# A two-layer MoE chain on one core: a strand's five output products in one go, and the issue order laid out anew

## The chip, the cores and the metric

The kernel runs on one core of a Trainium2 chip. The metric is device time in microseconds (us) for one execution, lower is better. The kernel before has two timed runs with a median of 1358.05 us.

## What is computed

Three stages follow each other. A causal convolution mixes each token with its six predecessors (softmax of seven taps for each of eight heads). Then two feed-forward layers run on 8192 tokens of width 192, with 2048 hidden channels each: `h = x @ w_in`, a function of `h` alone, then `g @ w_out`.

```python
x_unf = x_pad[:, idx, :].reshape(B, S, K, H, group)
out = np.einsum('hk,bskhg->bshg', w, x_unf)       # the convolution
g = h * np.clip(h + 3.0, 0.0, 6.0) / 6.0          # layer 1
P = a[0] + a[1] * h + a[2] * h2 + a[3] * h3       # layer 2
Q = 1.0 + np.abs(b[0]) * np.abs(h) + np.abs(b[1]) * h2
g = P / (Q + 1e-06)
```

## The kernel before

**Tiles and strands.** The tokens are cut into 16 blocks of 512 columns; the last is cut again into two units of 256, so there are 17 units. A unit takes 16 steps (the halves 8), and each step treats 128 hidden channels of a layer: a tile. Every number that enters a product is held as a high part and a low part (`h` and `l` in the tile names), and a product is the sum of three matmuls: high by high, low weight by high, high weight by low. TensorE's 128 rows are used as two halves of 64, called strands: `L` is rows 0 to 63 and `H` rows 64 to 127. Matmuls of the two strands run side by side. TensorE takes all of them from one queue in order, so a matmul that waits holds both strands.

**What happens to a tile.** `product_in` (`mm1` in layer 1, `mm3` in layer 2) makes `h` with nine matmuls of one strand into one of four PSUM banks. ScalarE (ACT), VectorE (DVE) and GpSimd (POOL) work out `g`; `hi1`/`hi2` (lines 953 and 1046, ACT) make its high part `g1h`/`g2h`, and `lo1`/`lo2` (lines 957 and 1052, POOL) its low part `g1l`/`g2l`. `product_out` then adds `g @ w_out` onto two accumulators: `acc..0` for output channels 0 to 127 (A) and `acc..1` for channels 128 to 191 with the low weights (B). For each strand it comes in two pieces: the piece for the high part, which issues A, A, B and needs only the high part, and the piece for the low part, which issues A, B.

**The fences.** Both strands add to the same accumulators, and two row halves must not write a bank at the same time. So where the strand changes on an accumulator, `fence_of` (line 635) puts an empty instruction on SP's queue that waits for the other strand's last matmul, and the first matmul of the new strand waits for that instruction. SP's queue also issues nearly all transfers: weights (`raw`, lines 733 to 737), tokens (`xn`, line 821), copies between partition halves (`X<-X`, `x1_dup` and `x2_dup`, line 894) and results (`out_dram`, lines 1094 and 1099). It is worked off in order too.

**The order.** Nothing of the order is written by hand. `make_plan` enters every operation with an engine, an assumed duration and a due time (`at`; the table `P["OFF"]` shifts it by operation). `Issue.order` plays the operations through a model with queues, rings of buffers and banks, and the instructions are issued by its start times. In that model `CROSS` (375 ns) is the distance that is kept between the strands on an accumulator; a fence takes no time of SP. Some entries on SP stand for several transfers: `load_w` for three (1950 ns), `load_x` for three (2400 ns), and copies and results are entered with 60 ns each. All transfers of an entry are issued at its start, one behind the other. A transfer issued there stands ahead of every fence that is planned later.

**The head.** `warm` runs 29 calls on zeros (5 over all rows, 12 of two matmuls with 512 columns, 12 of two with 192) before the convolution of blocks 0 and 1 (`conv0`, `conv1`), the transposes (`flip0`, `flip1`), and the first layer-1 products.

Of the kernel before, what the change touches and what calls it, by code (L numbers as in the profile page):

```python
# [15 lines left out]
SPAN = 58  # L16
C = 512
# [16 lines left out]
 'WARM': 29,  # L34
 'TH': 0.001,
 'DUP': 2600,
 'WPART': {'c0': 0.0497, 'v0': 0.0414, 'vs': 0.0403, 'h0': 0.2096, 'l0': 1.1533},
 'HEAD': 80.77,
 'TAIL': 205.47,
# [10 lines left out]
 'AHEAD': {'P': 63636833941.194, 'A': 527134343714.242, 'V': 3.0551887163097883e+19, 'G': 0.0, 'S': 999.0},  # L50
 'LOOK': {'P': 108, 'A': 139, 'V': 147, 'G': 63, 'S': 0},
 'BIAS': {'l1': -1.5284, 'dec': -4.5327, 'conv': -5.2656, 'out': -121.8403, 'x2': -83.2364},
 'OFF': {'sq': 2.5051,
         'q1': -34.3348,
         'q2': -49.934,
         'mm3': 1.398,
         'mm1': 2.9299,
         'mm4L': 3.5225,
         'mm4H': 2.7712,
         'tr': 18.9987,  # L60
         'mm2L': 4.3258,
         'mm2H': 5.2665,
         'A': 2.0453,
         't1': 1.7144,
         'u': -19.1188,
         'R': 46.5874,
         'RR': 3.1074,
         'hi2': 4.2135,
         'hi1': -20.696,
         'S': -21.1003,  # L70
         'lo2': 27.916,
         'lo1': -32.6451,
         'q': 7.2528,
         't2': 64.7646,
         't3': -9.1293,
         'w': -9.3652,
         'p2': 2.9972,
         'G': -37.509,
         'g': -9.5099,
         'cv': -34.3227,  # L80
         'x1ah': 45.5678,
         'x1al': -25.3374,
         'x1bh': 11.1259,
         'x1bl': -9.2318,
         'x2ah': -42.7502,
         'x2al': -101.0403,
         'x2mh': -17.8371,
         'x2mc': -53.8528,
         'x2ml': 72.7752,
         'oa': -65.1337,  # L90
         'oc': 11.2138,
         'os': 3.4069,
         'mm2lL': 4.9092,
         'mm2lH': 5.1772,
         'mm4lL': 3.5751,
         'mm4lH': -41.4037,
         '0.mm2L': -41.6908,
         '0.mm2lL': -85.6444,
         '0.mm2H': -21.0061,
         '0.mm2lH': -181.1908,  # L100
         '0.x2mh': -226.4626,
         '0.lo1': -47.901,
         '0.x2ml': 78.7106,
         '0.x2al': -138.5753,
         '0.x2mc': -132.4879,
         '0.mm1': -83.2957,
         '0.hi1': -166.5497,
         '0.g': -29.6109,
         '0.u': -157.145,
         '0.x2ah': -84.5959,  # L110
         'T.sq': -23.8172,
         'T.mm4lL': -110.3747,
         'T.mm4lH': -50.2917,
         'T.x2al': -5.029,
         'T.RR': -35.6781,
         'T.q2': -152.042,
         'T.oa': -153.8478,
         'T.lo2': 97.3004,
         'T.mm3': -180.9259,
         'T.q1': 0.5761,  # L120
         'T.A': -84.0279,
         'T.t3': -194.1138,
         'T.w': -176.0944,
         'T.G': -165.3819,
         'T.x2mh': -25.799,
         'T.x2ml': -100.5773,
         'T.hi2': -113.8752,
         'T.R': -115.1862,
         'T.p2': 21.7375,
         'T.tr': -148.8753,  # L130
         'T.q': -97.9184,
         'T.os': -90.2945,
         'T.mm4L': -58.7026,
         'T.mm4H': -180.8402,
         'T.x2mc': -189.2563,
         'trc': 1.5457,
         'x1d': 26.3031,
         'x2d': -34.7349,
         'x2e': 14.9362,
         '0.x2d': -16.7171,  # L140
         '0.x2e': -175.0551,
         'T.x2d': -72.3839,
         'T.x2e': -115.9305,
         'c.trc': -127.1013,
         'c.cv': 104.2546,
         'c.x1ah': -220.4013,
         'c.x1al': 77.084,
         'c.x1bh': 67.322,
         'c.x1bl': 59.1881,
         'c.x1d': -188.5031},  # L150
 'H1': 2,
 'H2': 3}
# [65 lines left out]

class Issue:
# [3 lines left out]
    CROSS = 375  # L223
# [12 lines left out]
    def lag(self, e, x):  # L236
        if e in "LH" and x in "LH":
            return 0 if e == x else self.CROSS
        p = lambda y: "P" if y in "LH" else y
        return self.DELAY.get(p(e) + p(x), 150)  # L240

    def graph(self):
# [5 lines left out]
        for k, op in enumerate(ops):  # L248
# [10 lines left out]
            assert all(key in written or key[0] == "X" for key in r), op  # L259
            for key in dict.fromkeys((*r, *w)):  # L260
# [19 lines left out]
                if key[0] == "X" and users[key]:  # L280
                    pred.setdefault(users[key][0], False)
# [16 lines left out]
    def order(self):  # L298
# [12 lines left out]
        def from_(k, e):  # L311
            if k in takes:
                return max(ready[k], min(idle[b][e] for b in idle))
            if ops[k][14] and ops[k][14][2]:
                last, x = lock.get(ops[k][14][0], (0.0, e))
                return max(ready[k], last + (self.CROSS if x != e else 0.0))
# [880 lines left out]
```

## Time and profile before

| | us |
|---|---|
| median of 2 runs | 1358.05 |
| lowest and highest | 1355.74, 1360.35 |
| the profiled execution, its own time | 1359.84 |
| its span, first to last instruction | 1358.0 |
| TensorE (PE) busy | 1294.3 |
| DVE, ACT, POOL busy | 1159.9, 1153.6, 1112.2 |

PE counts as busy as soon as one strand is; a matmul's end is modelled, so matmuls that follow each other on one strand overlap in the record. PEld is the loading of weights into the array. PEclk is the share of TensorE's clock that was granted. "SPq L635" as a releaser is a fence.

### The profile page before, as it was taken

To read this page: it belongs to the slowest core of one execution; us is meant where nothing else is said; L and a number is where in the kernel's file an instruction comes from. 1 tells how busy PE (TensorE), PEld (TensorE's weight loads), DVE (VectorE), ACT (ScalarE), POOL (GpSimd) and SP (SyncE) were. 2 spreads that over 40 slices of the span, in tenths; PEclk is the share of its full clock that TensorE was granted. 3 is DMA by queue.
4 is the path that set the end of the run, shared out by engine and by line. 5 is a ranking of instruction groups with operands and counts; after the bars stand their busy time and mean duration, and the time that the engine had idled before them with its cause. 6 is when DMAs were issued, how large, how long until landed. Compare 5 with 4: busy or idle time off the path is not lost.

```text
span 1358.0 us, 31232 instructions
## 1 busy us (share of the span) xinstructions
PE 1294.3 (95%) x11356; PEld 1132.5 (83%) x11356; DVE 1159.9 (85%) x1812; ACT 1153.6 (85%) x2121; POOL 1112.2 (82%) x948
## 2 busy tenths in 40 slices
PE   8888899999999999999999999999998999999998
PEld 6677688888877778888888989788997998999997
DVE  5777798898888979888998989898997998999985
ACT  3566798998888989888998989898997999999974
POOL 2578597898978889788997989898897898998963
PEclk7899999999999999999999999999999999999986
DMA  5443201102020200202012020200202110011010
GB/s 146 123 112 90 68 2 45 21 18 48 1 65 1 50 16 1 64 1 57 10 18 48 9 57 2 57 9 13 54 13 46 19 26 16 14 25 25 5 21 13
DMA packets 74466, 48.58 MB, mean 36 GB/s; under 512 B 43084, under 2 KB 64968, under 8 KB 74312
## 3 DMA queue, kind: packets, MB, share of 16 engines
q1 hardware_dynamic: 74152, 46.42, 14.8%
q8 instruction: 90, 1.47, 0.5%
q14 instruction: 64, 0.52, 0.1%
q10 hardware_dynamic: 160, 0.16, 0.1%
HBM read 20.34 MB, written 6.30 MB: 20 GB/s over the span
## 4 chain that ended last, share of the span: by engine, by line
PE 49%; ACT 21%; DVE 17%; SPq 5%; issue 5%; POOL 2%; DMA 0%; DVEq 0%; ACTq 0%; POOLq 0%
PE acc L628 25%; PE bank L628 23%; DVE T L1005 4%; ACT A L986 3%; ACT T L990 3%; ACT g1h L953 3%; DVE T L1017 2%; DVE S L1032 2%; ACT bank L1027 2%; ACT g2h L1046 2%; ACT A L1022 2%; DVE u L949 2%; DVE bank L1036 2%; ACT S L997 2%; ACT u L945 2%
## 5 line engine op out<-in xcount | busy, mean ns | idle before, releaser
L628 PE MATMUL bank<-X,Ih 64*128 64x512 f32 (+1 forms) x3264 | 926.8, 384 | 10.9 <-DVE T L1017 4.7
L628 PEld LDWEIGHTS bank<-X,Ih 64*128 64x128 f32 x3264 | 551.4, 187 | 67.0 <-DVE T L1017 12.5
L628 PE MATMUL bank<-X,Il 64*128 64x512 f32 (+1 forms) x1632 | 577.6, 379 | 0.0
L628 PE MATMUL acc<-g2h,O 64*128 64x512 f32 (+1 forms) x1728 | 473.0, 387 | 8.8 <-SPq L635 7.6
L628 PE MATMUL acc<-g1h,O 64*128 64x512 f32 (+1 forms) x1536 | 416.3, 381 | 9.7 <-SPq L635 8.9
L957 POOL TENSOR_TENSOR g1l<-u,g1h 128x512 fp32r<-128x512 f32 x240 | 310.8, 1297 | 77.1 <-ACT g1h L953 66.7
L1052 POOL TENSOR_TENSOR g2l<-T,g2h 128x512 fp32r<-128x512 f32 x255 | 330.5, 1298 | 46.4 <-ACT g2h L1046 34.2
L1011 POOL TENSOR_TENSOR S<-A,S 128x512 f32<-128x512 f32 x256 | 331.3, 1298 | 34.4 <-ACT S L997 19.3
L628 PE MATMUL acc<-g2l,O 64*128 64x512 f32 (+1 forms) x1152 | 344.9, 390 | 10.6 <-SPq L635 9.6
L628 PEld LDWEIGHTS acc<-g2h,O 64*128 64x128 f32 x1728 | 310.6, 191 | 27.4 <-SPq L635 9.7
L628 PE MATMUL acc<-g1l,O 64*128 64x512 f32 (+1 forms) x1024 | 303.2, 382 | 4.2 <-SPq L635 4.1
L628 PEld LDWEIGHTS bank<-X,Il 64*128 64x128 f32 x1632 | 293.5, 187 | 13.0
L628 PEld LDWEIGHTS acc<-g1h,O 64*128 64x128 f32 x1536 | 269.9, 186 | 30.7 <-SPq L635 13.3
L1005 DVE SCALAR_TENSOR_TENSOR T<-T,coef,bank 128x512 f32<-128x512 f32 x256 | 190.1, 743 | 47.8 <-ACT A L986 30.5
L628 PEld LDWEIGHTS acc<-g2l,O 64*128 64x128 f32 x1152 | 205.6, 191 | 28.7 <-SPq L635 14.6
L1017 DVE SCALAR_TENSOR_TENSOR T<-T,coef,bank 128x512 f32<-128x512 f32 x256 | 190.4, 745 | 20.5 <-ACT S L997 12.5
L1032 DVE SCALAR_TENSOR_TENSOR S<-S,bank 128x512 f32<-128x512 f32 x256 | 174.5, 683 | 32.3 <-ACT bank L1027 25.9
L990 ACT ACTIVATE T<-bank,coef 128x512 f32<-128x512 f32 x256 | 174.8, 684 | 23.5 <-PE bank L628 21.5
L628 PEld LDWEIGHTS acc<-g1l,O 64*128 64x128 f32 x1024 | 180.2, 185 | 16.9 <-SPq L635 4.5
L1036 DVE SCALAR_TENSOR_TENSOR bank<-T,coef,bank 128x512 f32<-128x512 f32 x256 | 191.7, 749 | 0.2
L949 DVE SCALAR_TENSOR_TENSOR u<-u,bank 128x512 f32<-128x512 f32 x240 | 163.2, 682 | 30.3 <-ACT u L945 26.8
L1041 DVE SCALAR_TENSOR_TENSOR T<-S,bank 128x512 f32<-128x512 f32 x256 | 175.1, 684 | 6.1
(90 smaller groups left out, 1733.7 us busy)
## 6 DMA issues: line engine op xcount, KB each, us to landing
X<-X SPq DMA_DIRECT2D x73, 256.0 KB, 3.3
raw<-in_moe_w_out_dram SPq DMA_DIRECT2D x16, 384.0 KB, 3.2
xn<-in_x_dram SPq DMA_DIRECT2D x28, 192.0 KB, 3.3
out_dram<-ov SPq DMA_DIRECT2D x60, 64.0 KB, 2.0
raw<-in_moe_w_in_dram SPq DMA_DIRECT2D x16, 192.0 KB, 3.6
raw<-in_moe_w_in_dram SPq DMA_DIRECT2D x16, 128.0 KB, 3.2
out_dram<-A SPq DMA_DIRECT2D x15, 128.0 KB, 2.0
raw<-in_moe_w_in_dram SPq DMA_DIRECT2D x16, 64.0 KB, 2.8
```

The source lines that it names most:

```text
L628: return nc.tensor.matmul(out=out, lhsT=lhsT, rhs=rhs, start=start, stop=stop, skip_group_check=True, **k)
L949: stt(out=t, in0=t, scalar=1.0, in1=h1.pop((b, i)), op0=ALU.min, op1=ALU.mult)
L953: act(out=g1[b, i][0], in_=v1[b, i], func=ACTF.Copy)
L957: nc.gpsimd.tensor_tensor(out=g1[b, i][1], in0=v1.pop((b, i)), in1=f32(g1[b, i][0]), op=ALU.subtract)
L990: act(out=tile2(b, i, "T"), in_=h2[b, i], func=ACTF.Copy, scale=coef[:, 3:4])
L1005: stt(out=d["T"], in0=d["T"], scalar=coef[:, 2:3], in1=h2[b, i], op0=ALU.add, op1=ALU.mult)
L1011: (nc.gpsimd if k else nc.vector).tensor_tensor(out=d["S"], in0=d["A"], in1=d["S"], op=ALU.add if k == 1 else ALU.mult)
L1017: stt(out=d["T"], in0=d["T"], scalar=coef[:, 1:2], in1=h2[b, i], op0=ALU.add, op1=ALU.mult)
L1032: stt(out=d["S"], in0=d["S"], scalar=c1, in1=r2[b, i], op0=ALU.add, op1=ALU.mult)
L1036: stt(out=r2[b, i], in0=v2[b, i]["T"], scalar=coef[:, 0:1], in1=r2[b, i], op0=ALU.add, op1=ALU.mult)
L1041: stt(out=d["T"], in0=d["S"], scalar=2.0, in1=r2.pop((b, i)), op0=ALU.subtract, op1=ALU.mult)
L1052: e.tensor_tensor(out=g2[b, i][1], in0=v2.pop((b, i))["T"], in1=f32(g2[b, i][0]), op=ALU.subtract)
```

## The change

`product_out` no longer has a piece for the high and one for the low part. One section issues all five products of a strand for a tile, A, A, A and then B, B, and needs both parts. `CROSS` becomes 212.7 ns, and lags between engines get an extra (`SLACK`: 98.6 ns from PE to another engine, 43.4 ns between others). Each transfer of `load_w` and `load_x` is an operation of its own with 645 ns on SP (weights of `w_out` 420, x with padding 1290), and copies and results are entered with 640, 490 and 430 ns instead of 60. A bank that passes from one engine to another keeps a lag in the model. `WARM` rises from 29 to 44 calls; the 15 more are pairs of 192 columns. The table of due times is new, without the entries that held for the first two and the last unit alone, and so are the rules that say how far an engine may look ahead. The number of products, evictions and vector operations stays as it was.

```diff
- 'WARM': 29,
+ 'WARM': 44,
...
+ 'CROSS': 212.7,
+ 'SLACK': [0, 98.6, 43.4]}
...
+        extra = P["SLACK"][0 if x in "LH" else 1 if e in "LH" else 2] if e != x and e != "S" and x != "S" else 0.0
+        return self.DELAY.get(p(e) + p(x), 150) + extra
...
-        at(t_load, None, "S", 1950, "load_w", *key, r=[("line_d", 0)], w=[("raw", key)], after=3400)
+        for j in range(parts):
+            at(t_load + 0.001 * j, None, "S", 645 if parts == 3 else 420, "load_w", *key, j, r=[("raw", key)] + [("line_d", 0)] * (t_load >= -62),
+               w=[("rl", key, j)], after=3600)
...
-                at(t, pick(z, "mm2" + e), e, o3, "product_out", 0, b, i, y, False, 
-                   d=D, r=[Hi] + [("out" + v, 0, c) for v in "hl" for c in cs], lock=ac, kind="l1")
-                at(t, pick(z, "mm2l" + e), e, o2, "product_out", 0, b, i, y, True, 
-                   d=D, r=[Lo] + [("outh", 0, c) for c in cs], lock=ac, kind="l1")
+                at(t, pick(z, "mm2" + e), e, o5, "product_out", 0, b, i, y,
+                   d=D, r=[Hi, Lo] + [("out" + v, 0, c) for v in "hl" for c in cs], lock=ac, kind="l1")
...
-            at(t, pick(z, ("x2d", "x2d", "x2e")[j]), "S", 60, "x2_dup", b, j, r=need + [X], w=[(f"x2d{j}", b)], after=P["DUP"], kind="x2", d=D)
+            at(t, pick(z, ("x2d", "x2d", "x2e")[j]), "S", 640, "x2_dup", b, j, r=need + [X], w=[(f"x2d{j}", b)], after=P["DUP"], kind="x2", d=D)
...
-        at(-100 + 45 * b if first else t - 8, None, "S", 2400, "load_x", b, r=[("line_d", 0)] if b else [], w=[xk(b)], after=1700)
+        for j in range(3):
+            at((-100 + 45 * b if first else t - 8) + 0.001 * j, None if first else f"ld{j}", "S",
+               645 if j or b * C % 4096 else 1290, "load_x", b, j, r=[xk(b)] + [("line_d", 0)] * (b == 1), w=[("xl", b, j)], after=1700)
...
-        seq = ((0, 0), (1, 128)) if lo else ((0, 0), (0, 256), (1, 128))
...
+        for j, parts in ((0, ((0, 0), (0, 256), (1, 0))), (1, ((0, 128), (1, 128)))):
+            for f, cs in tiles_of(l, u, i):
+                for lo, o in parts:
+                    count[l, u][j] += 1
+                    k = mm(acc[l, u][j], W[l]["O"][row(z), f, o:o + 128], (g1, g2)[l][u, i][lo][row(z), cs],
+                           count[l, u][j] == 1, count[l, u][j] == total[j])
+                    chain(k, fence.pop(j, None))
```

**Where instructions stand.** First PE's queue in the middle of the program, before. `bank` is the bank of a `product_in`; `acc_9011` and `acc_9012` are the A and B accumulators of a unit's layer 2, `acc_9159` and `acc_9160` those of another unit's layer 1; `g1` and `g2` are the layers' values.

```order
L628 MATMUL acc_9011<-g2h,O_129 128x512
L628 MATMUL bank_106<-X,Ih_124 128x512
L628 MATMUL acc_9011<-g2h,O_129 128x512
L628 MATMUL bank_106<-X,Il_125 128x512
L628 MATMUL acc_9012<-g2h,O_129 128x512
L628 MATMUL bank_106<-X,Ih_124 128x512
L628 MATMUL acc_9159<-g1l,O_126 128x512
L628 MATMUL bank_106<-X,Ih_124 128x512
L628 MATMUL acc_9160<-g1l,O_126 128x512
L628 MATMUL bank_106<-X,Il_125 128x512
```

The strand that adds takes the three products of a high part (A, A, B on layer 2) and goes on with the two of a low part of another unit (A, B). Now the same engine, same place, after; here `acc_8927` and `acc_8928` are A and B of layer 2.

```order
L585 MATMUL bank_105<-X,Ih_127 128x512
L585 MATMUL acc_8927<-g2h,O_129 128x512
L585 MATMUL bank_105<-X,Il_128 128x512
L585 MATMUL acc_8927<-g2h,O_129 128x512
L585 MATMUL bank_105<-X,Ih_127 128x512
L585 MATMUL acc_8927<-g2l,O_129 128x512
L585 MATMUL bank_105<-X,Ih_127 128x512
L585 MATMUL acc_8928<-g2h,O_129 128x512
L585 MATMUL bank_105<-X,Il_128 128x512
L585 MATMUL acc_8928<-g2l,O_129 128x512
```

All five products of a tile follow each other on one strand, three on A and then two on B.

Next PE's queue in the head, before: the last of block 2's convolution (`xn,band`) and the first product of layer 1 (`bank_105<-X,Ih_124`); `perm` rows are transposes of block 1.

```order
L874 MATMUL bank_105<-perm,X 128x58
L628 MATMUL bank_107<-xn,band 128x120 x2
L628 MATMUL bank_106<-xn,band 128x96
L628 MATMUL bank_107<-xn,band 128x120
L628 MATMUL bank_106<-xn,band 128x96
L628 MATMUL bank_107<-xn,band 128x120
L628 MATMUL bank_106<-xn,band 128x96 x2
L628 MATMUL bank_107<-xn,band 128x96 x2
L628 MATMUL bank_105<-X,Ih_124 128x512
```

Block 2's convolution stands between block 1's transposes and the first product. After, the same place:

```order
L836 MATMUL bank_105<-perm,X 128x58
L836 MATMUL bank_107<-perm,X 128x58
L836 MATMUL bank_105<-perm,X 128x58 x3
L836 MATMUL bank_107<-perm,X 128x58 x4
L836 MATMUL bank_108<-perm,X 128x58 x9
L585 MATMUL bank_105<-X,Ih_124 128x512
L585 MATMUL bank_105<-X,Il_125 128x512
```

The first product follows the transposes directly, and block 2's convolution has moved behind it.

Last SP's queue in the second half, transfers alone (fences stand between them but are not listed), before:

```order
L894 DMA X<-X 64x2x512 x2
L821 DMA xn<-in_x_dram 64x4x192
L821 DMA xn<-in_x_dram 64x192
L821 DMA xn<-in_x_dram 64x4x192
L894 DMA X<-X 64x2x512 x3
L1094 DMA out_dram<-ov 32x16x32 x4
L1099 DMA out_dram<-A 128x4x64
```

After:

```order
L856 DMA X<-X 64x2x512 x3
L782 DMA xn<-in_x_dram 64x4x192
L782 DMA xn<-in_x_dram 64x192
L782 DMA xn<-in_x_dram 64x4x192
L856 DMA X<-X 64x2x512 x2
L1055 DMA out_dram<-ov 32x16x32 x4
L1060 DMA out_dram<-A 128x4x64
```

The transfers are the same, and no transfer of another kind stands between the three of a block; what can now stand between them are fences.

## Rows read from the trace of the kernel before

**Rows 1.** The page: the span, and the engines' busy time.
```profile
span 1358.0 us, 31232 instructions
...
PE 1294.3 (95%) x11356; PEld 1132.5 (83%) x11356; DVE 1159.9 (85%) x1812; ACT 1153.6 (85%) x2121; POOL 1112.2 (82%) x948
```

**Rows 2.** Windows by stage: us, busy time by engine (instructions), granted clock, DMA share, GB/s.
```profile
680.00:816.00 136.00, 130.80 (x1155) 117.80 (x1153) 119.88 (x181) 121.23 (x224) 115.59 (x98) 0.99 0.16 33
...
1292.00:1358.00 66.00, 60.00 (x508) 56.81 (x508) 44.18 (x67) 37.79 (x69) 35.32 (x31) 0.76 0.06 16
```

**Rows 3.** Everything of line 635, the fences on SP's queue: who waited, us, times.
```profile
L635 SPq EVENT_SEMAPHORE  x1655: 17/17/17, 15.3 to 1353.2; - x184
...
  PEld acc L628: 42.1, 47
  PE acc L628: 30.2, 33
...
  PE bank L628: 4.6, 6
...
  PE bank L1076: 3.0, 2
```

**Rows 4.** Timeline 1031 to 1038 us: start, us, engine, line, tiles, idle before.
```profile
1032.12 1.26 SPq L894 DMA_DIRECT2D X<-X  x2
...
1033.48 2.38 SPq L821 DMA_DIRECT2D xn<-in_x_dram  x3
...
1035.97 0.61 PE L628 MATMUL acc<-g2h,O 64*128 64x512 f32 x1 [3.71 <-SPq L635]
...
1036.38 0.62 PE L628 MATMUL acc<-g2h,O 64*128 64x512 f32 x1
...
1036.81 0.62 PE L628 MATMUL acc<-g2h,O 64*128 64x512 f32 x1
```

**Rows 5.** Timeline 96 to 100 us, the weight loads in front of a fence.
```profile
96.54 0.59 SPq L733 DMA_DIRECT2D raw<-in_moe_w_in_dram  x1
...
97.83 1.34 SPq L735 DMA_DIRECT2D raw<-in_moe_w_in_dram  x1
...
99.29 0.50 PE L628 MATMUL acc<-g2l,O 64*128 64x512 f32 x1 [2.11 <-SPq L635]
```

**Rows 6.** Windows at the lower clock: after a stall, and in the head.
```profile
1036.20:1039.70 3.50, 3.50 (x21) 2.78 (x21) 0.00 (x0) 0.51 (x2) 1.31 (x2) 0.51 0.37 92
...
15.60:39.00 23.40, 20.15 (x134) 18.03 (x133) 13.17 (x29) 9.63 (x20) 5.46 (x7) 0.50 0.55 151
39.00:42.90 3.90, 3.90 (x24) 3.82 (x23) 2.19 (x4) 1.96 (x4) 1.66 (x3) 0.50 0.13 30
```

**Rows 7.** Timeline 700 to 712 us, PE alone: two products of one strand.
```profile
703.74 0.39 PE L628 MATMUL acc<-g2l,O 64*128 64x512 f32 x1
...
703.97 0.39 PE L628 MATMUL acc<-g2h,O 64*128 64x512 f32 x1
```

**Rows 8.** Timeline 0 to 70 us, PE alone: the head.
```profile
1.31 10.83 PE L628 MATMUL warm<-S 128*128 128x512 f32 x58 [1.31 <-POOL S L1144]
13.79 1.12 PE L628 MATMUL bank<-xn,band 64*128 64x120 f32 x8 [1.65 <-DVE bank L764]
...
35.90 0.35 PE L874 MATMUL bank<-perm,X 58*128 58x58 f32 x1 [1.12 <-SPq L635]
...
36.48 2.96 PE L628 MATMUL bank<-xn,band 64*128 64x120 f32 x19
39.02 0.79 PE L628 MATMUL bank<-X,Ih 64*128 64x512 f32 x1
```

**Rows 9.** Waits, the whole span: who for whom, us, times, longest.
```profile
POOL g1l L957 <- ACT g1h L953: 66.7, 62, 5.2
...
PEld acc L628 <- POOL g2l L1052: 4.1, 11, 0.7
```

**Rows 10.** The cores' view: span and mean granted clock.
```profile
core 0: 1358.0 us, clock 0.972
```

More of the change, by code (lines that the diff above doesn't have):

```diff
@@ new lines @@
+ 'BIAS': {'l1': 0.655, 'dec': -3.2567, 'conv': -2.0757, 'out': -68.933, 'x2': 12.7907},
+ 'OFF': {'mm1': -0.3963,
+         'mm3': 0.6728,
+         'mm2L': 1.6095,
+         'mm2H': 1.7392,
+         'mm4H': 1.9349,
+         'mm4L': 1.7642,
+         'u': -25.5386,
+         'g': -25.5649,
+         'hi1': 1.4623,
+         'lo1': -16.9858,
+         'A': 0.9323,
+         't1': 1.1357,
+         'sq': 1.029,
+         'S': -89.7777,
+         'q1': 4.7226,
+         'q2': -38.8906,
+         'q': -23.5736,
+         't2': 32.5165,
+         't3': -39.3835,
+         'R': 2.1496,
+         'RR': 2.9035,
+         'w': 7.3501,
+         'p2': 9.7635,
+         'G': -21.9836,
+         'hi2': 3.3361,
+         'lo2': 24.6885,
+         'x2ah': -38.4699,
+         'x2al': -5.4695,
+         'x2mh': -35.6159,
+         'x2ml': -45.0371,
+         'x2mc': -37.1715,
+         'oa': 22.1914,
+         'oc': 21.3387,
+         'os': -64.0888,
+         'tr': -1.3087,
+         'trc': -0.544,
+         'cv': -28.1883,
+         'x1ah': -5.6675,
+         'x1al': -13.6317,
+         'x1bh': -81.8593,
+         'x1bl': -31.9649,
+         'x1d': 49.2117,
+         'x2d': 47.847,
+         'x2e': 41.9904},
@@ L258, in graph @@
                 (adds if adding else ends).setdefault((home, unit), []).append(k)
-            assert all(key in written or key[0] == "X" for key in r), op
+            assert all(key in written or key[0] in SHARED for key in r), op
             for key in dict.fromkeys((*r, *w)):
@@ L313, in from_ @@
                 return max(ready[k], min(idle[b][e] for b in idle))
+            if k in uses and uses[k] in held:
+                x, last = held[uses[k]][2:]
+                return max(ready[k], last + self.lag(x, e)) if x != e else ready[k]
             if ops[k][14] and ops[k][14][2]:
@@ L350, in order @@
                 del idle[b]
-                held[takes[k]] = [b, dict.fromkeys(free, 0.0)]
+                held[takes[k]] = [b, dict.fromkeys(free, 0.0), e, 0.0]
                 args = (b, *args)
@@ L354, in order @@
             if k in uses:
-                b, rel = held[uses[k]]
+                b, rel = held[uses[k]][:2]
+                held[uses[k]][2:] = e, start + ns
+                touched |= set("AV")
                 for x in rel:
@@ L397, in weights @@
     def weights(t_load, t, kind, l, c):
+        parts = 3 if kind == "in" else 1
         key = (kind, l, c)
@@ L435, in make_plan @@
         half = cols_u < C
-        in_ns, o3, o2 = (2160, 720, 480) if half else (2040, 680, 453)
+        in_ns, o5 = (2160, 1200) if half else (2040, 1133)
         for i in range(steps[b]):
@@ L537, in make_plan @@
         if not b * C % 4096:
-            at(-101 + b if first else t - 9, None, "V", 207, "zero_x", b, w=[xk(b)])
-        at(-100 + 45 * b if first else t - 8, None, "S", 2400, "load_x", b, r=[("line_d", 0)] if b else [], w=[xk(b)], after=1700)
+            at(-101 + b if first else t - 9, None, "V", 207, "zero_x", b, r=[xk(b)], w=[("xl", b, 3)])
+        xl_ = [("xl", b, j) for j in range(3 + (not b * C % 4096))]
+        for j in range(3):
+            at((-100 + 45 * b if first else t - 8) + 0.001 * j, None if first else f"ld{j}", "S",
+               645 if j or b * C % 4096 else 1290, "load_x", b, j, r=[xk(b)] + [("line_d", 0)] * (b == 1), w=[("xl", b, j)], after=1700)
         z, step = "", 1.0
@@ L577, in make_plan @@
         at(-90 + k, None, "V", 75, "band_op", k, r=[("tap", 0)], w=[("line", 0)])
-    at(-62, None, "S", 400, "store_line", r=[("line", 0)], w=[("line_d", 0)], after=2200)
+    at(-62, None, "S", 400, "store_line", r=[("line", 0)], w=[("line_d", 0)], after=4100)
     for hf in range(2):
@@ L588, in make_plan @@
     for k in range(P["WARM"]):
-        at(-104 + 0.01 * k, None, "L", 800 if k < 5 else 200, "warm", k, r=[("idle", 0)], )
+        at(-104 + 0.01 * k, None, "L", 1300 if k < 5 else 227 if k < 17 else 113, "warm", k, r=[("idle", 0)], )
     return plan
@@ L725, in conv_moe_moe_kernel, with load_w @@
     raw = {}
-    def load_w(kind, l, c):
+    def load_w(kind, l, c, j):
         wi, wo = ((w_in1, w_out1), (w_in2, w_out2))[l]
-        t = sg.tile([128, 768], I32, tag="raw", name="raw")
+        if not j:
+            raw[kind, l, c] = [384, sg.tile([128, 768], I32, tag="raw", name="raw"), None]
+        t = raw[kind, l, c][1]
         if kind == "in":
```

205 lines of the change are left out of this document (48 added, 157 removed), and 10 rows, old and new, of the table P.

## The prediction

> **What bounds the kernel now.** I read the page first, then windows by stage, then the waits, and last the timeline around the longest waits. The page shows PE as the busiest engine [rows 1], and a window in the middle shows it busy for 130.80 of 136 us, against 121.23 for ACT, 119.88 for DVE and 115.59 for POOL [rows 2]. So PE sets the pace, with the others some 10% behind. But "busy" means that one strand works. On one strand a product follows the last after 0.23 us (703.74 to 703.97) though its record lasts 0.39 [rows 7].
>
> What makes PE wait is in the view of line 635. There are 1655 fences, and PE waited for one 33 + 6 + 2 = 41 times, for 30.2 + 4.6 + 3.0 = 37.8 us [rows 3]. The records' modelled ends hide 0.39 - 0.23 = 0.16 us of each, so both strands stood still for 37.8 + 41 x 0.16 = 44.4 us. (The weight loads' 42.1 us are largely the same stalls and are not added.) The timeline shows why. At 1032.12 SP issues two copies, at 1033.48 three loads of tokens that take 2.38 us to issue, and only then comes the fence; PE resumes at 1035.97 after 3.71 us [rows 4]. In the weight stage three issues from 96.54 to 99.17 hold a fence, and PE waits 2.11 us [rows 5]. The fence itself is never the slow thing: it stands in SP's queue behind transfers that have nothing to do with it.
>
> A long stall costs a second time. After the one of 3.71 us the granted clock is 0.51 for 3.5 us [rows 6], that is near 1.2 instead of 2.4 GHz, and products of a strand come 0.43 us apart (1036.38 to 1036.81) [rows 4]. Over the span the clock is 0.972 [rows 10], so 2 x 0.028 x 1358 = 76 us ran at the lower level. The head has 23.4 + 3.9 = 27.3 of these, from 15.6 to 42.9 [rows 6], and the last 66 us, at 0.76 [rows 2], 2 x 0.24 x 66 = 32. Some 17 us are left for short stretches behind stalls.
>
> **The change part by part.** *Transfers one by one (A).* The same transfers are issued on the same queue, but the plan now knows that each takes 0.6 us, and a fence planned between two of them is issued between them. A single issue takes 0.59 us [rows 5], so a fence should find at most one ahead of it, not three. It also has a longer lead: with A, A, A, B, B the last A product lies two products, 0.46 us, before the section's end, where it lay one, 0.23 us, before. Of a mean stall of 44.4 / 41 = 1.08 us I expect about a third to stay (0.6 less the lead, plus cases where SP itself waits for DVE or ACT before a copy). Value: -30 us. The bounds are 0, if fences land behind runs as before, and -44. The order speaks for some caution: the loads of a block still follow each other in threes.
>
> The rule that speaks against this term is in the Trainium skill, DMA: Bandwidth & Descriptors, section Issuing engines are not separate DMA queues: the time a sequencer needs to initiate a DMA is usually small beside the DMA. By it term A would be near nothing and the sum about 1347. The trace does not agree for this kernel: three issues took 2.6 us and held PE for 2.11.
>
> *The clock behind stalls (B).* In the 3.5 us at 0.51 PE ran 21 matmuls [rows 6]; two strands at 0.23 us would run 30. That is 9 x 0.115 = 1.0 us lost for each such stretch, and at most half of 17 us in all. If stalls over 2 us go, most of that goes: -5, bounds 0 and -8.
>
> *The head (C).* The first layer-1 product starts at 39.02, behind block 2's convolution and behind a fence that cost 1.12 us at 35.90 [rows 8]. In the new order it follows block 1's transposes. The convolution's 32 records at 2.96 / 19 = 0.16 us are 5 us at the low clock; they come back later beside other work. I take 4 us, and 1 us for the fence: -5. The longer warm-up adds 15 pairs of 192 columns, 192 / 512 x 0.23 = 0.09 us each, 1.3 us. The warm-up ended at 1.31 + 10.83 = 12.14 and the convolution began at 13.79 [rows 8], so the 1.65 us between cover it; without that cover it costs 1.3, at the low clock 2.6. Whether it keeps the clock up is the open point: PE ran at 0.50 from 15.6 to 39 although 20.15 of 23.4 us were busy with short matmuls [rows 6]. If the clock held, at most half of 20.15 + 3.9 us would go, -12. I take no gain, because the thin work that follows the warm-up is the same; bounds for the head +3 and -17.
>
> *Sections and crossing (D).* The built program has 1473 fences where it had 1655 [rows 3]: 182 fewer, or 91 fewer changes of strand with two fences each. At the planned 375 ns that is 34 us of one strand, 17 of both. On the other side the new order has 1007 places where a matmul follows one of its own strand, against 901; 106 x 0.23 = 24 us of one strand, 12 of both. Between -17 and +12 I take -3, near the middle.
>
> *Waiting for the low part (E).* A section now needs `g1l` or `g2l` from POOL, which comes 1.3 us after the high part. Nothing can be added in that time for this tile; the in-products of other tiles must cover it, and behind a waiting section on PE's queue everything waits, evictions on ACT and DVE next. Before, PE's loads waited for `g2l` 11 times for 4.1 us [rows 9], and POOL mostly waits itself (66.7 us for the high part). The plan knows the wait, so I take +2; below, 0; above, 4.1 / 11 = 0.37 us at all 544 tiles of both layers would be +200, which is a rival.
>
> Extra lags in the plan, the new ring rules and the new durations of ACT and POOL entries move starts in the model only; I cost them at nothing, since the same operations run for the same time, and the range holds what the layout makes of them.
>
> The sum for the profiled execution: 1359.84 - 30 - 5 - 5 - 3 + 2 = 1318.8. That run lay 1.8 us above the median of the two shown, so the forecast is 1317.
>
> **The rivals.** *The fences stay blocked.* The queue is still in order and still carries every transfer; if runs and fences collide as before because the real times drift from the plan's, A gives 8 instead of 30 and B 1: 1317 + 22 + 4 = 1343. For it: the triples in the order. Against it: in the stalls shown the fence came out right behind the last issue, so a place earlier in the queue helps at once.
>
> *Another engine takes over.* ACT is at 121.23 of 136; with 3% less time it is at 92%. If its in-order queue gives back half of what PE gains, the time is 1358 - 41 / 2 = 1338. Against it: shorter PE stalls also feed ACT earlier, and its own gaps are spread over the span.
>
> *POOL's low parts are late (slower).* Now each of 544 sections depends on POOL, busy 115.59 of 136 us [rows 2]. If a section waits 0.37 us in one of three cases, that is 181 x 0.37 = 67 us: 1317 + 67 = 1384. From about 0.08 us per section (44 us) on it eats the whole gain. For it: PE's queue is in order, and the early high piece that filled such gaps is gone. Against it: in the rows POOL waits for ACT and not PE for POOL.
>
> *More than forecast.* All 44 us of A, 8 of B, a head at full clock (-17), D at -10 and no E: 1358 - 79 = 1279.
>
> **How the numbers follow.** Forecast 0.54; fences stay blocked 0.17; another engine takes over 0.09; POOL late 0.06; more than forecast 0.14. The forecast's own range is 1298 to 1331. The range over the cases is 1283 to 1350: it leaves out the POOL case and the ends of the others. Two per cent, about what a measurement can tell here, is 1331. Faster by more: 0.54 + 0.14 = 0.68. Within: 0.17 + 0.09 = 0.26. Slower: 0.06.
>
> **What would show it.** If A is right, PE's idle time for fences falls from 37.8 us to 10 to 15, with no wait over 2 us. If B is right, the mean clock rises to about 0.98 with fewer short drops. If C is right, the first layer-1 product starts near 34 us. If E is small, PE's and its loads' waits for `g1l` and `g2l` stay under 10 us in all. The prediction is wrong if fence waits stay above 30 us, if POOL appears as a main releaser of PE, or if PE's waits go and the time does not, with ACT or DVE filling their windows instead.

## The result, and the profile after

The kernel after takes 1273.55 us (median of 2 runs, 1272.05 to 1275.05) against 1358.05: a ratio of 0.938 with a 95% interval of 0.930 to 0.946, so 84.5 us are gone. The forecast was 1317 with a range down to 1283; the time lies 43.5 us under the forecast and 9.5 us under the range. The profiled execution has a span of 1270.3 us.

First the page of the kernel after: span, busy time, and of part 4 the shares of the chain of work that ended last.

```profile
span 1270.3 us, 30971 instructions
...
PE 1247.7 (98%) x11386; PEld 1141.0 (90%) x11386; DVE 1153.7 (91%) x1812; ACT 1147.8 (90%) x2121; POOL 1110.9 (87%) x948
...
PE 79%; DVE 10%; ACT 4%; SPq 3%; issue 2%; POOL 1%; DMA 1%; DVEq 0%; ACTq 0%; POOLq 0%
```

The same row of the page of before, which [rows 1] leave out:

```profile
PE 49%; ACT 21%; DVE 17%; SPq 5%; issue 5%; POOL 2%; DMA 0%; DVEq 0%; ACTq 0%; POOLq 0%
```

The busy times of DVE, ACT and POOL are those of [rows 1] within 7 us; what went is time in which they and PE stood still. PE's busy time fell by 46.6 us; since PE counts as busy as soon as one strand is, that fits stretches in which one strand ran and the other waited, and time at the lower clock. PE carries 79% of the chain where it carried 49%: before, 38% of the chain ran through ACT and DVE, and the prediction, which took PE as the pace by its busy share, did not read that row.

Line 592, the fences, which answers to [rows 3]:

```profile
L592 SPq EVENT_SEMAPHORE  x1473: 17/17/17, 15.5 to 1265.4; - x185
...
  PEld acc L585: 11.6, 24
  PEld bank L1037: 5.4, 9
  PE acc L585: 4.9, 11
...
  PE bank L585: 2.2, 3
  PE bank L1037: 2.1, 4
  PE bank L836: 1.1, 2
```

PE waited 4.9 + 2.2 + 2.1 + 1.1 = 10.3 us in 20 waits. Before, the prediction summed 37.8 us in 41 waits; with the wait at the transposes of [rows 8] (1.1 us), which the sum above counts too, it is 38.9 in 42.

Windows of the same stretch in the middle, of the last 66 us, and of the head at the lower clock; they answer to [rows 2, 6]:

```profile
680.00:816.00 136.00, 136.00 (x1212) 125.97 (x1210) 127.42 (x197) 130.18 (x242) 126.70 (x107) 1.00 0.14 30
1204.00:1270.30 66.30, 59.52 (x584) 57.09 (x580) 48.53 (x77) 44.08 (x82) 40.25 (x35) 0.81 0.09 19
20.20:37.20 17.00, 14.88 (x101) 13.29 (x100) 11.02 (x22) 7.46 (x17) 5.43 (x5) 0.50 0.54 148
```

In the middle PE is busy for all 136 us, and every other engine works more in the same time than in [rows 2]: 127.42 for 119.88 on DVE, 130.18 for 121.23 on ACT, 126.70 for 115.59 on POOL. No engine took PE's place; all came closer together.

The head on PE, for [rows 8]:

```profile
1.31 13.10 PE L585 MATMUL warm<-S 128*128 128x512 f32 x88 [1.31 <-POOL S L1105]
14.25 1.06 PE L585 MATMUL bank<-xn,band 64*128 64x120 f32 x8
...
32.94 0.35 PE L836 MATMUL bank<-perm,X 58*128 58x58 f32 x1 [0.64 <-SPq L592]
33.05 0.79 PE L585 MATMUL bank<-X,Ih 64*128 64x512 f32 x1
```

The first layer-1 product starts at 33.05 us, 5.97 earlier than before.

Who waits for POOL's low parts and who holds POOL, for [rows 9]:

```profile
POOL g2l L1013 <- ACT g2h L1007: 28.9, 40, 2.3
...
POOL g1l L918 <- ACT g1h L914: 20.2, 31, 2.6
...
PEld acc L585 <- POOL g2l L1013: 1.7, 2, 1.1
...
PE acc L585 <- POOL g2l L1013: 1.3, 2, 0.9
...
PEld acc L585 <- POOL g1l L918: 0.5, 2, 0.3
```

PE's own idle time for the low part, which one section per strand needs earlier, is 1.3 us in all (0.3 before).

### The profile page after: what moved, and what is told of

It is laid out like the page before. It is cut to its first block, busy times and chain, and to the rows that moved or that the text cites. A ratio compares the mean times of both kernels' runs of the same rounds, so it can differ in the third digit from the quotient of the medians.

```text
span 1270.3 us, 30971 instructions
## 1 busy us (share of the span) xinstructions
PE 1247.7 (98%) x11386; PEld 1141.0 (90%) x11386; DVE 1153.7 (91%) x1812; ACT 1147.8 (90%) x2121; POOL 1110.9 (87%) x948
## 4 chain that ended last, share of the span: by engine, by line
PE 79%; DVE 10%; ACT 4%; SPq 3%; issue 2%; POOL 1%; DMA 1%; DVEq 0%; ACTq 0%; POOLq 0%
PE acc L585 42%; PE bank L585 36%; DVE bank L997 2%; DVE S L993 1%; DVE T L966 1%; DVE T L978 1%; DVE T L1002 1%; DVE u L910 1%; PE bank L836 1%; ACT A L947 1%; SPq L1055 1%; SPq L782 1%; ACT T L951 1%; ACT S L958 0%; PE bank L1037 0%
## 5 line engine op out<-in xcount | busy, mean ns | idle before, releaser
L585 PE MATMUL bank<-X,Ih 64*128 64x512 f32 (+1 forms) x3264 | 883.7, 378 | 3.3 <-DVE T L1002 1.9
L585 PEld LDWEIGHTS bank<-X,Ih 64*128 64x128 f32 x3264 | 543.8, 185 | 30.9 <-DVE T L1002 4.5
L585 PE MATMUL acc<-g2h,O 64*128 64x512 f32 (+1 forms) x1728 | 567.9, 385 | 3.2 <-SPq L592 3.0
L585 PE MATMUL bank<-X,Il 64*128 64x512 f32 (+1 forms) x1632 | 565.1, 376 | 0.0
L585 PE MATMUL acc<-g1h,O 64*128 64x512 f32 (+1 forms) x1536 | 496.8, 380 | 2.2 <-SPq L592 2.0
L585 PE MATMUL acc<-g2l,O 64*128 64x512 f32 (+1 forms) x1152 | 436.0, 381 | 1.3 <-POOL g2l L1013 1.3
L585 PE MATMUL acc<-g1l,O 64*128 64x512 f32 (+1 forms) x1024 | 380.8, 374 | 0.0
L918 POOL TENSOR_TENSOR g1l<-u,g1h 128x512 fp32r<-128x512 f32 x240 | 312.1, 1301 | 29.9 <-ACT g1h L914 20.2
L585 PEld LDWEIGHTS bank<-X,Il 64*128 64x128 f32 x1632 | 291.1, 185 | 10.5
L585 PEld LDWEIGHTS acc<-g1h,O 64*128 64x128 f32 x1536 | 274.4, 185 | 17.4 <-SPq L592 4.7
L585 PEld LDWEIGHTS acc<-g2l,O 64*128 64x128 f32 x1152 | 217.3, 189 | 10.5 <-POOL g2l L1013 1.7
L585 PEld LDWEIGHTS acc<-g1l,O 64*128 64x128 f32 x1024 | 188.9, 184 | 8.2 <-POOL g1l L918 0.5
```

The source lines that it names most:

```text
L585: return nc.tensor.matmul(out=out, lhsT=lhsT, rhs=rhs, start=start, stop=stop, skip_group_check=True, **k)
L918: nc.gpsimd.tensor_tensor(out=g1[b, i][1], in0=v1.pop((b, i)), in1=f32(g1[b, i][0]), op=ALU.subtract)
```

## Where the time was that the prediction did not see

The prediction's account had only the waits for fences. The waits of PE's weight loads for other engines in the kernel before show a second thing, which was read there and not priced:

```profile
PEld bank L628 <- DVE T L1017: 14.0, 27, 1.0
PEld bank L628 <- DVE T L1041: 10.6, 23, 1.6
PEld bank L628 <- DVE u L949: 9.4, 17, 1.6
```

A product of layer 1 or 2 cannot begin before DVE has done with a PSUM bank. All waits for DVE together are 39.8 us on the loads and 13.6 on the matmuls. The same view after:

```profile
PEld bank L585 <- DVE T L1002: 4.7, 10, 0.9
...
PEld bank L585 <- DVE u L910: 3.4, 5, 1.2
```

All waits for DVE are now 9.9 us on the loads and 3.8 on the matmuls.

To put both in one unit I took the start of every matmul in the trace, gave a product of 512 columns the 0.227 us in which one follows another on a strand (shorter ones in proportion, with the steps seen for them), and added up the stretches in which neither strand had work. Before, both stood still for 126.9 us of the span; after, for 52.3. The part in which the next matmul was released by a fence that came right behind a transfer's issue fell from 49.4 to 15.7 us (-34). The part with no fence at its end, in the body (more than 130 us from either end), fell from 33.2 to 3.0 us (-30). Half of the time in which one strand alone stood still fell from 78.8 to 64.4 (-14). Together -78 of 88 us of span; the rest lies at the two ends and in fences that were late for another reason. These sums are my own working from the trace, and no view prints them. They are a count of stalls and not yet a cause; the experiments are for that.

## The experiments

The first theory is that of the forecast: transfers that hold fences (A). Its rival is the layout, the new table of due times, which the prediction had costed at nothing. The kernel before is timed on the same chip each time; a ratio is to that. Runs e6, e9, e10 and e16 lie within 2% of before; what is said of them rests on intervals that leave out 1.

**1 and 2. Transfers alone, put in and taken out.** In e1 the plan and the order of all other engines are those of before; only SP's transfers keep a distance.

```diff
             nc.sync.dma_start(out=v[0:64], ...)
+            yield 645
...
+            if e == "S":
+                start = max(start, free)
+                free = start + {"x1_dup": 640, "x2_dup": 640, "out_sta": 490, ...}.get(f, ns)
```

> The kernel before with its plan and the order of every engine but SP kept; only SP's transfers are issued one by one, 640 ns apart, so that fences planned in between go between them. Theory 1 (fences blocked behind runs of transfers are the cause): PE's waits for fences fall from 37.8 us to 15 or less and the time falls by 30 to 45 us, to 1313 to 1328 us, short clock drops going too. Theory 2 (the new layout of the issue order is the cause, and transfers matter little): the time stays within 15 us of 1358.

Measured: 1326.29 us against 1355.06, ratio 0.978 (0.976 to 0.980), so -28.8 us, inside the band of theory 1. Line 635 of that run:

```profile
L635 SPq EVENT_SEMAPHORE  x1655: 17/17/17, 14.8 to 1321.6; - x184
...
  PEld acc L628: 22.3, 50
  PE acc L628: 7.3, 23
```

The number of fences is the same, the waits of PE on the accumulators are 7.3 us for 30.2 [rows 3], and all its waits for fences 12.0 for 38.9. The waits for DVE have not moved (loads 40.7 us).

In e2 the plan of after is kept, but the transfers of a `load_w`, `load_x` or `out_sta` go out together at the first one's start.

```diff
+            if f in ("load_w", "load_x", "out_sta"):
+                start = at_.setdefault((f, args[:-1]), start)
```

> The changed kernel with its plan and the order of every engine but SP kept; the transfers of a weight tile, of a block's tokens and of a result's four parts are issued together at the time of the first, as before the change. Theory 1: PE's waits for fences rise from about 9 us to 25 or more and the time rises by 20 to 30 us, to 1294 to 1304 us. Theory 2: within 10 us of 1274.

Measured: 1288.23, ratio 0.950 (0.948 to 0.951), 14.7 us more than after; PE's waits for fences are 23.5 us again for 10.3. The time lies between the two bands. Taken out, the distance costs half of what it gives when put in; two differences may account for that: here the copies still keep their distance, and half as many fences fall into an issue to begin with (counted below, runs 13 to 15).

**3. The warm-up.** e3 is after with 29 of the 44 warm-up calls; it leaves out 15 calls on zeros.

```diff
     def warm(kind):
+        if kind >= 29:
+            return
```

> The changed kernel with 29 warm-up calls issued instead of 44, nothing else moved. If the longer warm-up does something: the clock falls earlier in the head than 20.2 us after the start and the time rises by 2 to 6 us. If not: within 2 us of 1274.

Measured: 1273.81, ratio 0.940 (0.938 to 0.941): no difference, though the granted clock falls to the lower level at 15.4 us instead of 20.2, and over the span it is 0.978 where the profiled executions of after (this one and that of e18 below) have 0.984 and 0.981. The head on PE in that run:

```profile
1.31 10.76 PE L585 MATMUL warm<-S 128*128 128x512 f32 x58 [1.31 <-POOL S L1107]
14.53 1.20 PE L585 MATMUL bank<-xn,band 64*128 64x120 f32 x8 [2.46 <-DVE bank L727]
...
34.32 0.79 PE L585 MATMUL bank<-X,Ih 64*128 64x512 f32 x1
```

The gap before the convolution is 2.46 us instead of one that the longer warm-up fills, and the first layer-1 product comes 1.27 us later; a difference of that size can't be told from these times.

**4. The order inside a section.** e4 issues A, A, B, A, B in place of A, A, A, B, B, with the same plan.

```diff
-        for j, parts in ((0, ((0, 0), (0, 256), (1, 0))), (1, ((0, 128), (1, 128)))):
+        for part in (((0, 0, 0), (0, 0, 256), (1, 0, 128)), ((0, 1, 0), (1, 1, 128))):
```

> The changed kernel with the five products of a section issued A, A, B, A, B instead of A, A, A, B, B, nothing else moved. If the longer lead of the A fence matters (theory 3): the last A product is one product before the end, fences come 0.23 us later, and with some 700 changes of strand the time rises by 10 us or more. If the lead is covered anyway: within 5 us of 1274.

Measured: 1276.15 (1274.97 to 1281.64), ratio 0.942 (0.940 to 0.944). The lead that the last A product gets is worth some 2 us, and against the time of after in a later run (1274.89) it can hardly be told from nothing.

**5 and 6. The tables changed over.** e5 has the code and model of after with the due times and look-ahead rules of before; e6 the other way round, before with the tables of after.

```diff
- 'HEAD': 39.64, 'TAIL': 220.35, 'AHEAD': ..., 'LOOK': ..., 'BIAS': ..., 'OFF': ...
+ 'HEAD': 80.77, 'TAIL': 205.47, 'AHEAD': ..., 'LOOK': ..., 'BIAS': ..., 'OFF': ...
```

> The changed kernel's code and model with the due times and look-ahead rules of the kernel before (OFF, BIAS, AHEAD, LOOK, HEAD, TAIL); the order of all engines is laid out anew. Spaced transfers alone gave 29 of the 82 us. Theory M (the rest comes from the model: one section per strand and tile, real lags and durations): 1275 to 1300 us. Theory T (the rest comes from the table of due times that was found for it): 1320 us or more.

> The kernel before, code and model, with the new due times and look-ahead rules; pieces for the low part take the due time of the others. Theory T: 1300 us or less, since spaced transfers are all that is missing. Theory M: 1335 us or more.

Measured: e5 1400.9, ratio 1.033 (1.031 to 1.036); e6 1333.96, ratio 0.984 (0.982 to 0.986), that is 21 us faster than before with the transfers still in runs, the pieces still apart and the model unchanged. It misses theory T's band (1300 or less) and lies just under theory M's (1335 or more): the table is a part, not all of the rest. In e6 the waits of PE for fences are as long as ever, and those of its loads for DVE have gone:

```profile
PEld acc L590 <- SPq L597: 45.3, 52, 3.0
...
PEld bank L590 <- DVE T L1003: 2.6, 9, 0.4
PEld bank L590 <- DVE T L979: 2.3, 8, 0.9
...
PEld bank L590 <- DVE u L911: 1.9, 6, 0.5
```

In all 11.8 us for 39.8 on the loads, 2.5 for 13.6 on the matmuls. That answers to the part with no fence at its end. The old tables in the new model (e5) bring them back, 33.5 and 19.5 us, though the fences stay short at 11.3. But e5 is 127 us slower than after, and these waits are the smaller share: PE's busy time is 1350.9 us for 1247.7 on the same 11386 matmuls, and the clock over the span 0.955 for 0.984. What makes it so was not followed, so e5 shows that the new model needs the new table, and not what the table is worth.

**7 and 8. One section or two pieces, and a control.** e7 cuts the section of after into a high and a low piece again and lays the plan anew; e8 keeps the section and shifts each due time by a random amount of up to 0.1 step.

```diff
-                at(t, pick(z, "mm2" + e), e, o5, "product_out", 0, b, i, y, ...
+                at(t, pick(z, "mm2" + e), e, o5 * 0.6, "product_out", 0, b, i, y, False, ...
+                at(t, pick(z, "mm2" + e), e, o5 * 0.4, "product_out", 0, b, i, y, True, ...
```

> The changed kernel with a section cut in two again: a piece for the high part (A, A, B) that needs that part alone, and one for the low part (A, B); all else, tables included, stays, and the order is laid out anew. If one section per strand is what saves (theory S: fewer changes of strand, fewer fences): 1300 us or more. If it is not: within 12 us of 1274, or below it where the early high piece helps.

> A control: the changed kernel with each due time shifted by a random amount of up to 0.1 step. It shows how far the time moves when the order is laid out anew for no reason. Theories M and S: within 10 us of 1274. Theory T, if the table is finely tuned: 15 us or more above.

Measured: e7 1292.65, ratio 0.953 (0.951 to 0.956), between its two bands; e8 1294.94, ratio 0.955 (0.953 to 0.957). The control loses as much as the cut. A layout that is off by up to a tenth of a step costs 21 us in the one draw that was run, so the 19 us of e7 can't be put down to the pieces; what the one section is worth stays open. Nor do PE's waits show the loss of e8: they are 7.8 us for fences and 3.1 for DVE, both less than in after, while PE's busy time is 1272.6 us for 1247.7. It lies where one strand runs and the other stands, or at the lower clock (0.975 for 0.984).

**9 to 11. The new tables on one engine at a time**, in the code and model of before: the due times and look-ahead rules of DVE (e9, the entries for the first two and the last unit excepted), of ACT (e10), of PE (e11). POOL's alone were not tried.

```diff
-        t = base + d + P["OFF"].get(off, 0.0)
+        t = base + d + (NEW["OFF"].get(off.split(".")[-1] if off else off, 0.0) if eng in ENG else P["OFF"].get(off, 0.0))
```

> The kernel before, in which VectorE (DVE) alone takes its new due times, those for the first two and the last unit excepted; the order is laid out anew. Theory V (PE's waits for DVE, 13.6 us and 39.8 us at its weight loads before, 3.8 and 9.9 after, fall because DVE's order frees banks sooner): they fall below 8 and 20 us and the time falls by 15 us or more, to 1340 or less. If no single engine's order does it: 1340 to 1375 us, waits for DVE over 30 us.

> The kernel before, in which ScalarE (ACT) alone takes its new due times and look-ahead rules. DVE waited most for ACT. If ACT's order is what starves DVE, and DVE then PE: PE's waits for DVE fall below 8 us (loads 20) and the time falls to 1340 us or less. Theory V: 1345 us or more.

> The kernel before, in which TensorE alone takes its new due times and look-ahead rules. If PE's own order (which product stands where in its queue) makes the waits: PE's waits for DVE fall below 8 us (loads 20) and the time falls to 1340 us or less. Theory V: 1345 us or more.

Measured: e9 1376.28, ratio 1.014 (1.010 to 1.019); e10 1343.06, ratio 0.990 (0.987 to 0.993); e11 1400.65, ratio 1.032 (1.028 to 1.037). In e10 the waits came out as the theory of ACT says and the time 3 us above its bound of 1340. ACT's table alone takes most of PE's waits for DVE away: 8.7 us on the loads and 2.9 on the matmuls, while with DVE's own table they stay at 34.7 and 13.7. What it changes can be read from ACT's queue: for one tile of layer 2 the kernel before issues `t1` (T, line 990) ahead of `A` (line 986) for 243 of 256 tiles, the kernel after `A` (947) ahead of `t1` (951) for 240. On `A` hangs the longer chain (S, q, R, RR, w, p2, G), on `t1` the shorter one (t2, t3). In every run the waits go with this order: `t1` comes first for 235 to 252 tiles in before, e5, e9, e11 and e16, and their matmuls wait 13.6 to 19.5 us for DVE (e1 and e15, with the order of before, 13.4 and 14.4); `A` comes first for 234 to 240 in after, e6, e10 and e12, and they wait 2.5 to 3.8 (in the other runs with the order of after at most 8.0, in e13). The reading that fits is that DVE's chain ends late where ACT starts it late, and PE waits for DVE's end. It is argued and not shown: these two operations alone were not tried, ACT's table moves others and its look-ahead too, and of the 21 us of e6 e10 has 15.

**12. Both together.** e12 is e6 with the distance of e1.

> The kernel before with the new tables for all engines (1334 us alone) and SP's transfers issued one by one (29 us alone). If the two gains are of different waits, they add up: 1300 to 1310 us, with PE's waits for fences near 12 us and for DVE near 3. If they overlap: 1315 us or more. What is then left to 1274 us belongs to the new durations, lags and sections in the plan with which the tables were found.

Measured: 1301.2, ratio 0.959 (0.956 to 0.962). The two gains add, and a little more: 28.8 + 21 were expected, some 57 us came. Of the 27.6 us from here to after, the count of stalls has 13 behind transfers' issues (28.7 against 15.7 us).

**13 to 15. Transfers moved to the far side of fences.** A plan tells in advance where a fence will be wanted within the 0.6 us of an issue: 74 of 270 transfers in the plan of before with its distances kept, 72 in that of e12, 39 of 268 in that of after. These runs issue such a transfer right behind the fence.

```diff
+                near = [g for g in gaps if start < g < start + 2000]
+                spots = [start] + [g + 1 for g in near if g + 1 < start + 1200]
+                room = lambda t: min(600, min([g - t for g in near if g > t], default=600))
+                start = max(spots, key=lambda t: (room(t), -t))
```

> The kernel after with its plan kept; only SP's transfers move. A transfer behind which a fence is planned within 0.6 us is issued right behind that fence instead, at most 1.2 us later (46 of 695 move; before the move 39 have such a fence, after it none). Theory: in the kernel after both strands still stand still for 15.7 us because a fence finds an issue ahead of it; the planned collisions are a part of this, so the time falls to 1262 to 1269. Rival: the collisions that are left come from the drift between the plan's times and the real ones; then moving the planned ones changes nothing, 1271 to 1276.

> The kernel before with the new tables and its transfers issued one by one (1301.2 in the run of that version), and now also moved behind fences by the same rule (59 move). That version stood still for 28.7 us behind issues, the kernel after for 15.7. Theory: these 13 us are planned collisions; 1288 to 1295. Rival: they are drift, since the plan of this version does not know how long an issue takes; 1299 to 1303.

> The kernel before with its own plan, transfers one by one (1326.3 in the run of that version) and moved behind fences by the same rule. Theory: of the 23 us that are left behind issues half goes, 1312 to 1318. Rival, drift: 1324 to 1328. If it comes under 1317, the transfers alone carry the whole forecast.

Measured: e15 1309.13, ratio 0.965 (0.962 to 0.968); e14 1281.64, ratio 0.944 (0.940 to 0.948); e13 1270.61, ratio 0.937 (0.934 to 0.939). The collisions were mostly planned ones and not drift: with the old table this alone takes 17 us more off e1, with the new one 20 off e12, a little past what was expected of either. Line 635 of e15:

```profile
  PEld acc L628: 5.0, 18
...
  PE acc L628: 0.7, 1
```

Of 30.2 us that PE waited on the accumulators 0.7 are left. And yet the chain of e15 (first row) is nearly that of before, while that of e14 (second), which differs by the table alone, is close to that of after:

```profile
PE 52%; ACT 23%; DVE 17%; issue 4%; SPq 2%; POOL 1%; DMA 0%; DVEq 0%; ACTq 0%; POOLq 0%
PE 81%; DVE 7%; ACT 6%; SPq 2%; issue 2%; POOL 1%; DMA 1%; DVEq 0%; ACTq 0%; POOLq 0%
```

So the transfers and the table are two causes. (The share is not the table's alone: e5, with the old tables in the new model, has 71% on PE.) In e13 the time falls between the theory's band and the rival's, and its interval overlaps that of after: by itself it shows no gain.

**16. A control for before.** e16 shifts the due times of before at random, as e8 did with those of after.

> The kernel before, every due time of its table shifted by a random amount of up to 0.1 of a step, as was done to the kernel after (which lost 21 us by it); nothing else changed. If the new layout gains because its table is tuned to its model more finely than the old one, the kernel before loses little here: 1355 to 1365. If both are tuned alike, and the gain lies in what the model knows, it loses as much: 1372 to 1385.

Measured: 1379.98, ratio 1.017 (1.013 to 1.020), 24 us slower. Both tables are tuned alike to their models, the second of the two answers, as far as one draw each can tell. So a version that has to lay its plan anew may carry some 20 us of loss, and clear are only runs that keep a plan (e1 to e4, e13, e15, e17, and e12 and e14 beside e6) or that won in spite of it (e6, e10).

**17 and 18. A version that beats both.** e17 is e13 with the fences of convolutions and transposes counted too; e18 is after, unchanged, beside it.

```diff
+            if f in ("conv1", "flip1", "out_trc1", "out_tr1"):
+                gaps.append(start)
```

> The kernel after, its transfers moved behind fences as in e13, and now the fences of convolutions and transposes, which cross strands in a bank, count as well. In e13 PE's weight loads still wait 4.6 us at the result transposes (L1037), 4.5 us at the token transposes (L836) and 3.8 us for in-products' banks behind fences. Theory: half of these 13 us is an issue ahead of the fence and goes: 1262 to 1267. Rival: at these places other work of the same strand or DVE is late next, and the time stays at 1269 to 1273.

> The kernel after, unchanged, on the same chip as e17, for a direct comparison of the two: 1272 to 1275. If e17 lies more than 0.3% below it, moving the transfers pays on top of the change.

Measured: e17 1267.95 (1264.82 to 1268.85), e18 1274.89 (1274.07 to 1276.80); ratios 0.934 (0.931 to 0.937) and 0.940 (0.938 to 0.943) to the same runs of before. The six times of e17 lie under the five of e18, 0.5% apart. The fences of e17:

```profile
L592 SPq EVENT_SEMAPHORE  x1473: 17/17/17, 15.8 to 1262.0; - x185
...
  PEld acc L585: 5.2, 12
...
  PE acc L585: 1.9, 4
  PE bank L836: 1.6, 1
  PE bank L1037: 1.1, 1
```

PE waits 1.9 + 1.6 + 1.1 = 4.6 us for fences, 5.9 less than in e18 (10.5), and 7.2 for DVE instead of 3.7: part of what is won at the fences may be spent there. The time came out between the two bands that were written down.

## Why the prediction was wrong

**The step that failed** is the sentence "Extra lags in the plan, the new ring rules and the new durations of ACT and POOL entries move starts in the model only; I cost them at nothing, since the same operations run for the same time". Its last clause left the layout to the range, which did not hold it. It left out the new table as well, which stood in the change, and term D, the only one on the order, took -3 us. The table by itself, in the old code and model, gives -21 us (e6); on top of transfers that are kept clear it gives 1309.13 - 1281.64 = 27 us (e15 to e14). The operations do run for the same time, but when DVE gives PE a bank depends on the order: these waits (13.6 us on matmuls, 39.8 on loads) stood in the view of waits and had no term, and with the new table most of them go. Under it lies the first step, "So PE sets the pace": the busy share said so, but PE had only 49% of the chain. A mean of "no gain, no loss" for a new layout was a choice without a row behind it.

**A, the transfers: right in mechanism and sign, and in size for what it described.** Forecast -30, measured -28.8 for single issues (e1). Its lower bound of -44 was "all of it", and placing the transfers clear of fences does reach that: 1356.14 - 1309.13 = 47 us (e15). The plan of after lies between, with half as many planned collisions and, by the count of stalls, 34 us less stillness behind issues. PE's waits for fences, forecast at 10 to 15 us, are 10.3, and the longest of a matmul is 1.4 us ("no wait over 2 us"). Here 28.8 us hung on the distance between issues alone. The rule of the Trainium skill that was weighed there (DMA: Bandwidth & Descriptors, Issuing engines are not separate DMA queues: initiating is usually small beside the DMA) does not make A near nothing, as the prediction had it. The trace agrees with the sentence, 0.606 us of issue beside 3.3 us to landing (line 782, last section); it speaks of the transfer, and not of what stands behind the issue on the same queue.

**B, the clock behind stalls: right in what was to be seen.** In the trace of before the clock drops to the lower level at five places between 49 and 1040 us, 17 us in all; after, it does not drop between 37.3 and 1245 us, and in e1, where the transfers alone keep a distance, one such drop is left in the body, at 534 us. The mean is 0.984 (forecast "about 0.98"), and 2 x 0.016 x 1270 = 41 us ran at the lower level instead of 76. What this alone is worth was not tried.

**C, the head: right in where the first product starts.** The first layer-1 product was forecast near 34 us and came at 33.05, 5.97 earlier for a term of 5; the low stretch there is 17 us long instead of 27.3. "I take no gain" for the warm-up holds by e3. What the earlier start is worth at the end was not tried.

**D, sections and crossing: the value of e4 is about 2 us, that of the single section is open** (e7 beside e8).

**E, the low part: small, as forecast.** +2 was taken; matmuls wait 1.3 us for `g2l` and loads 1.7 + 0.5 for `g2l` and `g1l`, where they had waited 0.3 and 4.1 + 0.5 ([rows 9] have the 4.1). Whether waiting sections delay others was not tried.

**The rivals.** "The fences stay blocked" fell with the 10.3 us. "Another engine takes over" fell: PE has 79% of the chain, and ACT's window of 130.18 of 136 us goes with PE's 136.00. "POOL late" fell with E. "More than forecast" (1279) had the right side and an amount 5 us off, but by the wrong sum: it put 12 us on a full clock in the head, where the clock stayed low for 17 us, and 7 on D, which no run shows, and nothing on the table. That it came so near is luck.

What stays open: the 8 us between e14 (1281.64) and after, or the 11 to e13, whose transfers are moved by the same rule as e14's. In them the single section, the lags and durations of the new model and the head lie together, with what e14 loses by a table that was found for another model.

## What to carry to other kernels

Where instructions that others wait for share an in-order queue with transfers, count how many of the waits are planned: issues of 0.6 us ahead of fences cost this kernel 47 us in all, and keeping transfers apart and on the far side of the fences won it without touching another engine. A new issue order is not a neutral part of a change: look at the chain that ends last and at all waits of the bounding engine, not only at those that the change speaks of; and even these do not price it in full, as e8 shows. And before an undone part is believed, run a control that lays the plan anew without undoing anything; here that alone cost 21 and 24 us in one draw each.

## What the hardware showed that was not expected

Most issues on SP take about the same time, and so they can be planned around. The transfers of tokens after, in ns (least, median, most), and from issue to landing in us:

```profile
L782 SPq DMA_DIRECT2D xn<-in_x_dram x45: 595/606/1238, 2.1 to 974.6; - x45
...
DMA to landing us min/median/max: 2.7/3.3/5.5
```

The fences themselves take 17 ns (17/17/17 in every view of them above).

The clock in the head did not follow the length of the warm-up alone. Three runs with one window each, 12 to 45 us: e18, which is after, then e3 and e13.

```profile
12.00:45.00 33.00, 27.56 (x223) 23.80 (x221) 22.18 (x44) 17.07 (x35) 13.18 (x14) 0.74 0.55 143
```

```profile
12.00:45.00 33.00, 26.35 (x169) 22.19 (x168) 20.75 (x41) 15.54 (x32) 11.71 (x12) 0.64 0.51 136
```

```profile
12.00:45.00 33.00, 26.79 (x186) 22.34 (x185) 19.80 (x39) 14.49 (x31) 11.83 (x12) 0.65 0.53 139
```

With 44 calls after has a granted clock of 0.74 in this stretch and e3 with 29 has 0.64, but e13, with 44 calls and the same queue on PE, has 0.65. The time of e3 (1273.81) lies within 1.1 us of both of after (1273.55 and 1274.89).
